# A gated linear attention and feed-forward kernel: all attention products in one block of 64x64 quarters of the array

## The chip, the cores and the metric

The kernel runs on one core of a Trainium2 chip. Its engines are called as in the profile: PE (TensorE, matmuls; PEld is its weight load), DVE (VectorE), ACT (ScalarE), POOL (GpSimd) and SP (SyncE, which here only issues transfers). The metric is the device time of one execution in microseconds, as a median over runs.

## What is computed

```python
# attention: 4 batches, 8 heads, 768 steps, head dimension 48
for t in range(S):
    state = alpha[:, :, t, :, None] * state + einsum('bhd,bhe->bhde', k[:, :, t], v[:, :, t])
    y[:, :, t] = einsum('bhd,bhde->bhe', q[:, :, t], state)
x = y.transpose(0, 2, 1, 3).reshape(3072, 384)
# feed-forward: d_model 384, d_ff 1024
out = ((x @ w1) * (x @ w2)) @ w3 @ w_out
```

The attention is a recurrence with a decay per step and dimension. The weights come as 64-bit floats and are turned into fp32 on the chip.

## The kernel before, in words

The sequence is cut into chunks of 128 steps: 6 per batch (NCH), 24 in all (N). One loop, `for n in range(N + 1)`, runs over them; its iteration n does the scores of chunk n and the output of chunk n-1, and prepares chunks n+1 to n+4. Between the attention steps it converts weights (`convert`) and, from n = 7 on, computes tiles of the first two feed-forward products (`run`, line 515, here called gate work): 3 half-tiles an iteration or fewer, and none at n = 9, 13, 17 and 21, by the table `pieces`. After the loop the feed-forward is finished: remaining gates, `w3 @ w_out` folded into one matrix, and the last product. The matmuls of line 515 make up most of the kernel.

For one chunk:
- `logs` and `decays`: logarithms of alpha (ACT), their running sums by a matmul (lines 340, 343, 346), exponentials e (ACT, 349 and 350).
- `decayed` (line 359, DVE): k and q times e, into qk. Lines 381 and 383 transpose qk on PE and copy it from PSUM to qkT (ACT). There the even head of a pair lies on partitions 0 to 47, the odd one on 64 to 111: the head's parity i sets its half of the partitions, and so its half of PE's rows. j numbers the four pairs.
- scores k times q, masked so that a query meets only keys up to its own step: up to n = 7 by full 128x128 products (line 454) and two DVE masks (457); from n = 8 (TURNED) on by quarters of the array (line 430): the block of early keys against all 128 queries and the block of late keys against the 64 late queries. An odd head's blocks lie turned by a half, and four DVE operations mask them (line 440).
- the output, in two PSUM tiles y[i]: the state of earlier chunks times q (line 474), and scores times v. The values are in the early chunks one product per head over all 128 keys (line 485). From n = 8 on the first half of the queries is done between the next chunk's scores (`attend_low`, line 419) and the second half after the transposes (line 482). A copy of the odd heads' v with its halves exchanged (vt, line 167, POOL) serves that.
- ACT copies y to x (line 489), and SP stores it to DRAM (xd) with two transfers per chunk; later x is gathered from there for the feed-forward (line 501).
- `outer` (line 393) makes the chunk's own k times v, and `advance` (lines 410 to 412, POOL) decays the state every second chunk.

All PSUM tiles come from one pool of eight banks; a bank is taken again when its readers are done. Each engine works through its instructions in order. The order written in the loop is kept on PE; the framework places the instructions of the other engines, and `issue_after` holds some back. SP issues nearly all loads in order; POOL issues the v loads of chunks 3 to 7 and the small transfers for the decay.

Of the kernel before, what the change touches and what calls it, by code (L numbers as in the profile page):

```python
# [10 lines left out]
FP32 = mybir.dt.float32  # L11
FP32R = mybir.dt.float32r
I32 = mybir.dt.int32
# [3 lines left out]
ALU = mybir.AluOpType  # L17
# [31 lines left out]
def kernel(  # L49
# [24 lines left out]
    G = 3  # L74
# [3 lines left out]
    AHEAD = 3  # L78
    LATE = 10
    PAIRED = 8  # L80
    TURNED = 8
    assert D <= DP and DM % C == 0 and DF % CW == 0 and S % C == 0 and N % G == 0
    assert DM <= 512 and TG <= 512

    def pool(name, bufs, stack=ctx, **kw):
        return stack.enter_context(tc.tile_pool(name=name, bufs=bufs, **kw))
# [34 lines left out]
    xd = [dram.tile([DM, TG], FP32, name=f"xd{g}") for g in range(NG)]  # L121
# [5 lines left out]
    vts = [p1.tile([C, NP, DP], FP32, name=f"vt{i}") for i in range(2)]  # L127
# [28 lines left out]
    def load_v(n):  # L156
        if n < N:
            st["v", n] = vs[n % len(vs)]
            (nc.gpsimd if 2 < n < 8 else nc.sync).dma_start(out=st["v", n][:, :, 0:D], in_=rows(v, n))

    def turned(n):
        return TURNED <= n < N

    def turn_v(n):
        if turned(n):
            for half in range(2):
                nc.gpsimd.tensor_copy(out=vts[n % 2][ds(DP * half, DP), :, 0:D],
                                      in_=st["v", n][ds(DP * (1 - half), DP), 1::2, 0:D])

    spare = tr[0].tile([C, 3 * KM * TG], FP32R, tag="x3", name="x3")[:].bitcast(FP32)  # L170
    sums2 = spare[:, 0:4 * C].rearrange("p (e s t) -> p e s t", e=2, s=2)
# [13 lines left out]

    w12 = [p.tile([C, 3, 2, KM, CW], FP32R, name=f"w12{i}") for i, p in enumerate((w12ap, const))]

    made = work.tile([C, 2, NP, C], FP32, tag="ms", name="ms")
    utri, after = made[:, 0, 0, :], made[:, 0, 1, :]

    sums = p1.tile([C, 2, C], FP32R, name="sums")
    signs = p1.tile([C, 2, C], FP32R, name="signs")
    keep = p1.tile([C, C], I32, name="keep")
    keep_turned = p1.tile([C, 2, DP], I32, name="keep_turned")
    qks = [p1.tile([C, 2, H, DP], FP32, name=f"qk{i}") for i in range(3)]
    Ts = [p1.tile([C, NP, DP], FP32, name=f"T{i}") for i in range(2)]
    decs = [p1.tile([C, 3, NP], FP32, name=f"dec{i}") for i in range(2)]
# [5 lines left out]
    nc.gpsimd.tensor_copy(out=sums[:, 1], in_=utri)  # L203
    nc.vector.memset(rebias, -(1023.0 - 127.0) * 2.0 ** 23)

    nc.vector.tensor_scalar_mul(keep, utri, -1.0)
    keep_bc = keep[:, None, :].to_broadcast([C, NP, C])
    for half in range(2):
        nc.gpsimd.tensor_copy(out=keep_turned[ds(DP * half, DP), 1 - half], in_=keep[ds(DP * half, DP), ds(DP * half, DP)])
    nc.gpsimd.memset(keep_turned[DP:, 1], -1)  # L210
    for x in qks:
        nc.vector.memset(x[:, :, :, D:], 0.0)
    make_identity(nc, ident)
# [55 lines left out]
    weights, begun, thirds, done = deque(), deque(), deque(), []  # L269
# [29 lines left out]
    later = deque()  # L299
# [112 lines left out]
        mark["pool"] = nc.gpsimd.tensor_tensor(Ts[0][:, :, 0:D], st.pop(("T", n - 1)),  # L412
                                               dec[:, :, None].to_broadcast([C, NP, D]), op=ALU.mult).ins

    def attend_low(n, jj, i, half):

        s, w = ds(DP * i, DP), (vts[n % 2] if i else st["v", n])
        h = half * NP // 2 + jj
        nc.tensor.matmul(st["y", n][0][i][ds(DP * half, DP), jj, 0:DP], w[s, h if i else 2 * h, :],  # L419
                         st["ms", n][s, i, h, 0:DP], start=(n % NCH == 0 and jj == 0), stop=True, skip_group_check=True)  # L420

    def turned_scores(n):

        qkT = st["qkT", n]
        sc = [bank().rearrange("p (j c) -> p j c", j=NP) for _ in range(2)]
        for j in range(NP):
            for part in range(2):
                for i in range(2):
                    r, t = ds(DP * i, D), slice(DP * part, C)
                    nc.tensor.matmul(sc[i][ds(DP * (part ^ i), DP), j, t], qkT[r, 0, j, ds(DP * part, DP)],  # L430
                                     qkT[r, 1, j, t], start=True, stop=True)
            if turned(n - 1):
                for i in range(2):
                    attend_low(n - 1, j % 2, i, i ^ (j < 2))
        ms = work.tile([C, 2, NP, C], FP32, tag="ms", name="ms")
        for i in range(2):
            r = ds(DP * i, DP)
            low, high = (keep_turned[r, 0], keep_turned[:, 1]) if i else (keep[r, 0:DP], keep[:, DP:])
            for x, mask, t in ((slice(DP * i, DP * (i + 1)), low, slice(0, DP)), (slice(0, C), high, slice(DP, C))):
                masked = nc.vector.tensor_tensor(ms[x, i, :, t].bitcast(I32), sc[i][x, :, t].bitcast(I32),  # L440
                                                 mask[:, None, :].to_broadcast([x.stop - x.start, NP, DP]),
                                                 op=ALU.bitwise_and)
        ends_of_part1[0] = mark["ms", n] = masked.ins
        st["ms", n] = ms

    def scores(n):
        if turned(n):
            return turned_scores(n)
        qkT = st["qkT", n]
        sc = [bank().rearrange("p (j c) -> p j c", j=NP) for _ in range(2)]  # L450
        for j in range(NP):
            for i in range(2):
                r = ds(DP * i, D)
                nc.tensor.matmul(sc[i][:, j, :], qkT[r, 0, j, :], qkT[r, 1, j, :], start=True, stop=True)  # L454
        ms = work.tile([C, 2, NP, C], FP32, tag="ms", name="ms")
        for i in range(2):
            masked = nc.vector.tensor_tensor(ms[:, i].bitcast(I32), sc[i].bitcast(I32), keep_bc, op=ALU.bitwise_and)  # L457
        ends_of_part1[0] = mark["ms", n] = masked.ins
        st["ms", n] = ms

    HP = NP // 2

    def attend_state(n):
        qkT = st.pop(("qkT", n))

        y = [bank()[:, 0:HP * C].rearrange("p (j c) -> p j c", c=C) for _ in range(2)]
        st["y", n] = y, [(half * HP + j, i, y[i][ds(DP * half, DP), j, :])
                         for j in range(HP) for i in range(2) for half in range(2)]  # L470
        if n % NCH:
            for j, i, to in st["y", n][1]:
                r = ds(DP * i, D)
                nc.tensor.matmul(to, Ts[n % 2][r, j, :], qkT[r, 1, j, :],  # L474
                                 start=(j % HP == 0), stop=False, skip_group_check=True)

    def attend(n):
        (y, heads), ms, vc = st.pop(("y", n)), st.pop(("ms", n)), st.pop(("v", n))
        for j, i, to in heads:
            if turned(n):  # L480
                w = vts[n % 2][:, j, :] if i else vc[:, 2 * j, :]
                nc.tensor.matmul(to[:, DP:], w, ms[:, i, j, DP:], start=False,  # L482
                                 stop=(j % HP == HP - 1), skip_group_check=True)
            else:
                nc.tensor.matmul(to, vc[:, 2 * j + i, :], ms[:, i, j, :], start=(n % NCH == 0 and j % HP == 0),  # L485
                                 stop=(j % HP == HP - 1), skip_group_check=True)
        x = work.tile([C, HP, 2, C], FP32, tag="x", name="x", bufs=4)
        for i in range(2):
            copied = nc.scalar.copy(x[:, :, i], y[i])
        ends_of_part1[1] = copied.ins  # L490
        x = x.rearrange("p j i t -> p (j i) t")

        g, c = divmod(n, G)
        to = xd[g].rearrange("(b h d) t -> b d h t", b=2, d=D)
        for half in range(2):
            later.append((to[half, :, :, ds(c * C, C)], x[ds(DP * half, D)]))


    def load_x(g, queue=nc.sync):
        st["xT", g] = xp.tile([C, KM, TG], FP32, tag="xT", name="xT")  # L500
# [27 lines left out]
    ends_of_part1 = [None, None]  # L528
    pending, late = deque(), False
# [159 lines left out]
    for n in range(N + 1):  # L689
# [14 lines left out]
                fetch(raws)  # L704
        if n >= FIRST:
            load_v(n + 2)
        if n:
            attend_state(n - 1)
        if n < N:
            scores(n)  # L710
        else:
            for j in range(NP):
                for i in range(2):
                    attend_low(n - 1, j % 2, i, i ^ (j < 2))
        transposed(n + 1)
        if n == 1:
            decays(3)
# [8 lines left out]
        if n - 2 in begin and n > FIRST:  # L726
            g, tiles = begin[n - 2]
# [16 lines left out]
        if n < N - 2 and n != FIRST:  # L744
            with after_marks(*marks):
                convert(2 if early else 1, raws)
        advance(n)
        turn_v(n)
        if n:
            attend(n - 1)  # L750
        outer(n)
        if n > FIRST:
            third(ready)
# [35 lines left out]
    late = True  # L789
# [12 lines left out]
    low, high = range(FH), range(FH, KF)  # L802
# [74 lines left out]
```

## Time and profile before

| what | us |
|---|---|
| median of 3 runs | 465.93 |
| lowest and highest | 465.54, 466.16 |
| the profiled execution | 464.49 |
| its span in the profile | 462.8 |
| masks of early chunks, DVE L457, 16 operations | 10.3 |
| masks of later chunks, DVE L440, 64 operations | 26.6 |
| vt copies, POOL L167, 32 operations | 17.8 |
| x copies, ACT L489, 48 operations | 15.7 |
| matmuls of line 515 on PE, all shapes | 346.3 |

A line of the profile's groups gives the source line, the engine, the operation, the tiles written and read, shapes and count, then busy time, mean ns of one, and the idle time just before them with what ended it. The chain of waits follows the work that ended last from its end to its start; a piece of it has a start, a length and a line. An fp32 matmul shows as two passes, so eight matmuls are x16. A timeline lists instructions by engine with start and length; lengths of neighbours overlap, since a matmul's or copy's time counts until its last write.

### The profile page before, as it was taken

What the parts mean: (1) busy time and instruction counts of PE and PEld (TensorE: products, weight loads), DVE (VectorE), ACT (ScalarE), POOL (GpSimd) and SP (SyncE); (2) the same over time, 40 slices, a digit from 0 to 9 for tenths busy, and PEclk for the clock granted to TensorE, in tenths of its full rate; (3) what the DMA queues carried; (4) which work ended last, traced back from release to release, by engine and by line L of the source; (5) the groups of instructions that cost most, each with busy time, mean ns of one, the idle gap of its engine ahead of it and who ended that gap; (6) DMA issues with size and microseconds to landing.
All of it is one profiled execution on the core that took longest, in us unless ns stands there. A gap on an engine that the chain in (4) does not pass through costs nothing.

```text
span 462.8 us, 11150 instructions
## 1 busy us (share of the span) xinstructions
PE 446.9 (97%) x4296; PEld 423.2 (91%) x4296; DVE 371.7 (80%) x610; ACT 276.4 (60%) x544; POOL 95.1 (21%) x186
## 2 busy tenths in 40 slices
PE   4998999999999999999999999999999999999996
PEld 2675699898999989999999999999999999999996
DVE  2779997999979988999998999997542967776671
ACT  4685975767658563988875676764545443333430
POOL 6234232325414430121221201212010000000000
PEclk9999999999999999999999999999999999999999
DMA  9999999999999974466856446412115875665511
GB/s 173 254 208 228 261 224 192 248 209 219 184 227 193 234 165 138 130 224 212 235 178 196 146 128 177 149 52 86 51 48 153 243 210 180 186 178 159 166 51 52
DMA packets 148869, 80.37 MB, mean 174 GB/s; under 512 B 97392, under 2 KB 138608, under 8 KB 148816
## 3 DMA queue, kind: packets, MB, share of 16 engines
q1 hardware_dynamic: 143040, 64.44, 57.3%
q0 software_dynamic: 5776, 15.22, 11.0%
q8 instruction: 34, 0.56, 0.5%
q14 instruction: 19, 0.16, 0.1%
HBM read 57.58 MB, written 22.06 MB: 172 GB/s over the span
## 4 chain that ended last, share of the span: by engine, by line
PE 88%; DVE 4%; DMA 4%; ACT 2%; issue 1%; SPq 0%; DVEq 0%; ACTq 0%
PE bank L515 72%; DMA kq<-in_q_dram 3%; PE bank L381 3%; PE bank L430 3%; PE bank L482 2%; PE bank L474 2%; PE bank L340 1%; PE bank L393 1%; PE bank L346 1%; PE bank L454 1%; PE bank L343 1%; PE bank L419 1%; DVE qk L359 1%; DVE ms L457 1%; PE bank L485 1%
## 5 line engine op out<-in xcount | busy, mean ns | idle before, releaser
L515 PE MATMUL bank<-x,w 128*128 128x384 f32 x1152 | 210.2, 337 | 1.7 <-ACT qkT L383 1.1
L515 PEld LDWEIGHTS bank<-x,w 128*128 128x128 f32 x1152 | 200.2, 188 | 4.1 <-ACT qkT L383 1.4
L515 PE MATMUL bank<-w3o,ab 128*128 128x384 f32 x576 | 100.2, 336 | 0.0
L515 PEld LDWEIGHTS bank<-w3o,ab 128*128 128x128 f32 x576 | 99.9, 188 | 0.0
L540 ACT ACTIVATE bank<-bank 128x384 f32<-128x384 f32 x96 | 45.6, 476 | 43.4 <-PE bank L515 43.1
L524 ACT ACTIVATE t<-bank 128x384 f32<-128x384 f32 x64 | 31.9, 499 | 54.9 <-PE bank L515 54.9
L590 POOL DMA_DIRECT2D abd<-ab x45 | 25.8, 573 | 137.9 <-DVE ab L576 121.3
L383 ACT COPY qkT<-bank 128x512 f32<-128x512 f32 x48 | 26.2, 596 | 24.8 <-PE bank L381 24.8
L641 DVE TENSOR_TENSOR ab<-abl,ab 128x1024 fp32r<-128x1024 f32 x24 | 29.3, 1223 | 12.3 <-ACT ab L640 12.3
L640 ACT ACTIVATE ab<-abl 128x1024 fp32r<-128x1024 f32 x24 | 25.5, 1061 | 20.2 <-PE bank L515 18.4
L515 PE MATMUL bank<-wo,w3T 128*128 128x384 f32 x192 | 35.9, 334 | 0.0
L576 DVE TENSOR_TENSOR ab<-bank,r 128x384 f32<-128x384 f32 x44 | 24.1, 548 | 12.5 <-PE bank L515 6.3
L515 PEld LDWEIGHTS bank<-wo,w3T 128*128 128x128 f32 x192 | 33.5, 188 | 0.0
L249 ACT ACTIVATE power<-power,rebias 128x512 uint32<-128x512 uint32 (+1 forms) x36 | 25.3, 701 | 12.6 <-DVE power L248 12.4
L359 DVE TENSOR_TENSOR qk<-kq,e 128x768 f32<-128x768 f32 x24 | 23.1, 964 | 11.3 <-ACT e L350 7.9
L526 DVE SCALAR_TENSOR_TENSOR o<-bank,t 128x384 f32<-128x384 f32 x24 | 13.4, 557 | 23.0 <-issue 13.7
L642 DVE SCALAR_TENSOR_TENSOR ab<-ab,abl 128x1024 fp32r<-128x1024 f32 x24 | 29.2, 1217 | 0.0
L526 DVE SCALAR_TENSOR_TENSOR r<-bank,t 128x384 f32<-128x384 f32 x40 | 22.0, 550 | 6.8 <-PE bank L515 3.4
L251 DVE SCALAR_TENSOR_TENSOR mant<-mant,rest 128x512 f32<-128x512 uint32 (+1 forms) x36 | 23.4, 649 | 3.7 <-ACT rest L244 3.7
L252 DVE SCALAR_TENSOR_TENSOR power<-raw,power 128x512 uint32<-128x512 uint32 (+1 forms) x36 | 23.5, 653 | 2.4 <-ACT power L249 2.4
L253 DVE TENSOR_TENSOR mant<-mant,power 128x512 f32<-128x512 f32 (+1 forms) x36 | 23.6, 655 | 0.5
L244 ACT ACTIVATE rest<-raw 128x512 f32<-128x512 uint32 (+1 forms) x36 | 23.3, 649 | 0.0
(102 smaller groups left out, 675.2 us busy)
## 6 DMA issues: line engine op xcount, KB each, us to landing
abl<-abd SPq DMA_DIRECT2D x24, 512.0 KB, 4.7
abd<-ab POOLq DMA_DIRECT2D x45, 192.0 KB, 3.2
raw<-in_moe_w_dram SPq DMA_DIRECT2D x64, 128.0 KB, 3.4
raw<-in_moe_w_dram SPq DMA_DIRECT2D x12, 512.0 KB, 5.8
xT<-xd POOLq DMA_DIRECT2D x9, 576.0 KB, 4.7
kq<-in_k_dram SPq DMA_DIRECT2D x24, 192.0 KB, 5.2
kq<-in_q_dram SPq DMA_DIRECT2D x24, 192.0 KB, 5.4
xd<-x SPq DMA_DIRECT2D x48, 96.0 KB, 3.9
```

The lines of the kernel that those rows point to most:

```text
L249: nc.scalar.activation(power, power, AF.Relu, scale=2.0 ** 23, bias=rebias)
L359: mark["qk", n] = nc.vector.tensor_mul(qks[n % 3][:, :, :, 0:D], st.pop(("kq", n)), st.pop(("e", n)).rearrange("p i (h d) -> p i h d", h=H ...
L383: mark["qkT", n] = nc.scalar.copy(qkT[:, :, :, ds(DP * half, DP)], tp[half]).ins
L515: nc.tensor.matmul(p, w[part][i], x[part][i], start=start and part == parts[0] and i == 0, stop=stop and part == parts[-1] and i == n - 1, ...
L524: nc.scalar.activation(t, p1, AF.Copy, scale=(1.0 + 1.0 / P) * scale)
L526: nc.vector.scalar_tensor_tensor(to, p2, scale, t, op0=ALU.mult, op1=ALU.add)
L540: nc.scalar.activation(p, p, AF.Copy, scale=1.0 + 1.0 / P)
L576: nc.vector.tensor_mul(ab, p, r[0])
L590: (nc.gpsimd if late else nc.sync).dma_start(out=abd[g][:, f, :], in_=ab)
L640: nc.scalar.activation(t[:, 0], ab, AF.Copy, scale=1.0 - 2.0 ** -13)
L641: nc.vector.tensor_sub(t[:, 1], ab, t[:, 0].bitcast(FP32))
L642: nc.vector.scalar_tensor_tensor(t[:, 2], t[:, 0].bitcast(FP32), -1.0 - 1.0 / P, ab, op0=ALU.mult, op1=ALU.add)
```

## The change

TURNED falls away; all chunks use quarters of 64x64. LQ = 3 is new. For each head pair j and parity i:
- Scores go to the quarter (i, i): rows of the parity, outputs on the parity's partitions. Early keys against all queries go to one bank (two halves e = 0 and 1 of the queries side by side), late keys against late queries to another.
- The masked scores ms have the form [128, 3, 4 pairs, 64]: first-half queries (DVE mask), second-half queries for early keys (no mask needed, an ACT copy), second-half queries for late keys (DVE mask). Both halves of the keys lie on the partitions of the head's parity.
- State and values of pairs j = 0 to 2 go to the quarters (i, 1-i) and into one PSUM tile of three pairs; those of pair 3 go to (i, i), like the scores, and into another. The values of all queries are done here, so lines 419, 482 and 485 become one place.
- `attention(n)` interleaves the two lists, state and values of pairs 0 to 2 on one side, scores of n and then state and values of pair 3 on the other, by costs 2 and 1 for 128 and 64 columns.
- vt now serves both parities: both its halves hold the other half of v, and it is made for every chunk.
- The copy to x and its store stay where the values stood in the loop. A chunk is stored with four transfers (three pairs or one pair, for each half) instead of two.

```diff
-    TURNED = 8
+    LQ = 3
     def turn_v(n):
-        if turned(n):
-            for half in range(2):
-                nc.gpsimd.tensor_copy(out=vts[n % 2][ds(DP * half, DP), :, 0:D],
-                                      in_=st["v", n][ds(DP * (1 - half), DP), 1::2, 0:D])
+        if n < N:
+            for i in range(2):
+                nc.gpsimd.tensor_copy(out=vts[n % 2][ds(DP * i, DP), :, 0:D],
+                                      in_=st["v", n][ds(DP * (1 - i), DP), i::2, 0:D])
...
+    keep = p1.tile([C, DP], I32, name="keep")
+    keep_bc = keep[:, None, :].to_broadcast([C, NP, DP])
...
+    def attend(n):
+        ms, vc, vt, qkT = st.pop(("ms", n)), st.pop(("v", n)), vts[n % 2], st.pop(("qkT", n))
+        y = [bank()[:, 0:x * C].rearrange("p (j c) -> p j c", c=C) for x in (LQ, NP - LQ)]
+        first, state = set(), n % NCH > 0
+        def add(j, i, w, x, t):
+            at = j >= LQ
+            to = y[at][ds(DP * (i if at else 1 - i), DP), j - LQ * at, t]
+            nc.tensor.matmul(to, w, x, start=(at, i) not in first, stop=True, skip_group_check=True)
+            first.add((at, i))
+        def steps(heads):
+            for j in heads * state:
+                yield 2, [(j, i, Ts[n % 2][ds(DP * i, D), j, :], qkT[ds(DP * i, D), 1, j, :], slice(0, C)) for i in range(2)]
+            for j in heads:
+                yield 2, [(j, i, vt[DP:, j, :] if i else vc[0:DP, 2 * j, :], ms[ds(DP * i, DP), 0:2, j, :], slice(0, C))
+                          for i in range(2)]
+            for j in heads:
+                yield 1, [(j, i, vc[DP:, 2 * j + 1, :] if i else vt[0:DP, j, :], ms[ds(DP * i, DP), 2, j, :], slice(DP, C))
+                          for i in range(2)]
...
+        def copied():
+            x = work.tile([C, NP, C], FP32, tag="x", name="x", bufs=4)
+            for a, b in zip(y, (x[:, 0:LQ], x[:, LQ:])):
+                ends_of_part1[1] = nc.scalar.copy(b, a).ins
+            g, c = divmod(n, G)
+            to = xd[g].rearrange("(j i d) t -> i d j t", i=2, d=D)[:, :, :, ds(c * C, C)]
+            for half in range(2):
+                s = ds(DP * half, D)
+                later.append((to[1 - half, :, 0:LQ], x[s, 0:LQ]))
+                later.append((to[half, :, LQ:], x[s, LQ:]))
...
+    def scores(n):
+        qkT = st["qkT", n]
+        sc = [bank().rearrange("p (e j c) -> p e j c", e=2, j=NP), bank()[:, 0:NP * DP].rearrange("p (j c) -> p j c", j=NP)]
+        def score(x):
+            j, late = x
+            for i in range(2):
+                r, to = ds(DP * i, D), ds(DP * i, DP)
+                q = qkT[r, 1, j, ds(DP * late, DP)] if late else qkT[r, 1, j, :].rearrange("p (e c) -> p e c", e=2)
+                nc.tensor.matmul(sc[1][to, j, :] if late else sc[0][to, :, j, :], qkT[r, 0, j, ds(DP * late, DP)], q,
+                                 start=True, stop=True)
+        def masked():
+            ms = st["ms", n] = work.tile([C, 3, NP, DP], FP32, tag="ms", name="ms")
+            for e, x in ((0, sc[0][:, 0]), (2, sc[1])):
+                last = nc.vector.tensor_tensor(ms[:, e].bitcast(I32), x.bitcast(I32), keep_bc, op=ALU.bitwise_and)
+            mark["ms", n] = ends_of_part1[0] = last.ins
+            nc.scalar.copy(ms[:, 1], sc[0][:, 1])
+        return [(2 - late, score, (j, late)) for j in range(NP) for late in range(2)], masked
+    def attention(n):
+        low, high = attend(n - 1) if n else ([], [])
+        done = None
+        if n < N:
+            own, done = scores(n)
+            high = own + high
+        low, high, at = deque(low), deque(high), [0, 0]
+        while low or high:
+            k = 0 if not high or low and at[0] <= at[1] else 1
+            cost, f, x = (low, high)[k].popleft()
+            at[k] += cost
+            f(x)
+        if done:
+            done()
...
-        if n:
-            attend_state(n - 1)
-        if n < N:
-            scores(n)
...
+        attention(n)
         transposed(n + 1)
...
         advance(n)
         turn_v(n)
         if n:
-            attend(n - 1)
+            st.pop(("x", n - 1))()
         outer(n)
```

More of the change, by code (lines that the diff above doesn't have):

```diff
@@ L159, in load_v @@
             (nc.gpsimd if 2 < n < 8 else nc.sync).dma_start(out=st["v", n][:, :, 0:D], in_=rows(v, n))
-    def turned(n):
-        return TURNED <= n < N
     def turn_v(n):
-        if turned(n):
-            for half in range(2):
-                nc.gpsimd.tensor_copy(out=vts[n % 2][ds(DP * half, DP), :, 0:D],
-                                      in_=st["v", n][ds(DP * (1 - half), DP), 1::2, 0:D])
+        if n < N:
+            for i in range(2):
+                nc.gpsimd.tensor_copy(out=vts[n % 2][ds(DP * i, DP), :, 0:D],
+                                      in_=st["v", n][ds(DP * (1 - i), DP), i::2, 0:D])
     spare = tr[0].tile([C, 3 * KM * TG], FP32R, tag="x3", name="x3")[:].bitcast(FP32)
@@ L186 @@
     w12 = [p.tile([C, 3, 2, KM, CW], FP32R, name=f"w12{i}") for i, p in enumerate((w12ap, const))]
-    made = work.tile([C, 2, NP, C], FP32, tag="ms", name="ms")
-    utri, after = made[:, 0, 0, :], made[:, 0, 1, :]
+    made = work.tile([C, 3, NP, DP], FP32, tag="ms", name="ms").rearrange("p a j c -> p (a j c)")
+    utri, after = made[:, 0:C], made[:, C:2 * C]
     sums = p1.tile([C, 2, C], FP32R, name="sums")
     signs = p1.tile([C, 2, C], FP32R, name="signs")
-    keep = p1.tile([C, C], I32, name="keep")
-    keep_turned = p1.tile([C, 2, DP], I32, name="keep_turned")
+    keep = p1.tile([C, DP], I32, name="keep")
     qks = [p1.tile([C, 2, H, DP], FP32, name=f"qk{i}") for i in range(3)]
@@ L204 @@
     nc.vector.memset(rebias, -(1023.0 - 127.0) * 2.0 ** 23)
[L206 to L210, printed above, removed]
+    for i in range(2):
+        nc.vector.tensor_scalar_mul(keep[ds(DP * i, DP)], utri[ds(DP * i, DP), ds(DP * i, DP)], -1.0)
+    keep_bc = keep[:, None, :].to_broadcast([C, NP, DP])
     for x in qks:
@@ L413, in advance @@
                                                dec[:, :, None].to_broadcast([C, NP, D]), op=ALU.mult).ins
[L415 to L422, printed above, removed]
-        qkT = st["qkT", n]
[L425 to L451, printed above, removed]
-            for i in range(2):
[L453 to L496, printed above, removed]
+    def attend(n):
[16 more added lines that the diff above has]
+                          for i in range(2)]
+        def act(x):
+            for y in x:
+                add(*y)
+        def copied():
[8 more added lines that the diff above has]
+                later.append((to[half, :, LQ:], x[s, LQ:]))
+        st["x", n] = copied
+        return *([(k, act, x) for k, x in steps(list(h))] for h in (range(LQ), range(LQ, NP))),
@@ L706 @@
             load_v(n + 2)
-        if n:
-            attend_state(n - 1)
-        if n < N:
-            scores(n)
[L711 to L714, printed above, removed]
+        attention(n)
         transposed(n + 1)
```

## Prediction

> **What bounds the kernel.** I read the page's busy times first, then its forty slices, then the chain that ended last.
>
> ```profile
> PE 446.9 (97%) x4296; PEld 423.2 (91%) x4296; DVE 371.7 (80%) x610; ACT 276.4 (60%) x544; POOL 95.1 (21%) x186
> ...
> PE   4998999999999999999999999999999999999996
> ...
> DVE  2779997999979988999998999997542967776671
> ...
> PE 88%; DVE 4%; DMA 4%; ACT 2%; issue 1%; SPq 0%; DVEq 0%; ACTq 0%
> ```
>
> PE is busy 446.9 of 462.8 us and holds 88% of the chain; its granted clock is 1.0 in every slice. From 184 us on, PE runs the feed-forward without a gap (30.0 of 30.0 us in each stretch up to 430), and the change doesn't touch that. So the question is how much earlier the last attention (n = 24, at 183 us) is done. A table of busy time by stretch gives PE's idle time before: 9.7 us in 0:50, 0.3 in 50:70, 1.1 in 70:90, 0.6 in 90:130, none in 130:170, 0.5 in 170:190. After 50 us, PE work removed is time won, unless a new wait eats it. Before 50 us something else decides:
>
> ```profile
> 39.74 7.11 DMA kq<-in_q_dram
> 46.97 0.96 DVE qk L359
> 47.93 1.20 DVE ms L457 x2
> ```
>
> In this stage the chain runs from a load of k and q over VectorE's work (the masks included) to the next load; PE is not in it.
>
> **PE's work per chunk.** The chain of one full iteration (n = 15), with start, length and what ran:
>
> ```profile
> 119.48 0.60 PE bank L474 x16
> ...
> 121.19 0.64 PE bank L381 x16
> 121.83 0.61 PE bank L482 x16
> 122.45 0.45 PE bank L393 x16
> 122.90 0.71 PE bank L515 x3
> ```
>
> Each fp32 matmul counts as two passes. L474 (state: N=128, four passes on each of four quarters) takes 0.60; L485 (values of early chunks: N=128, eight passes on each column half) takes 1.02 in the chain. So four passes of 128 cost 0.42, one 0.105, and the start-up is 0.18. L482 (N=64, eight passes per half) takes 0.61: a pass of 64 costs (0.61-0.18)/8 = 0.054. Test: scores and first-half values (120.08 to 121.19, 1.11 us) put 8 passes of 128 and 4 of 64 on the quarters (i,i): 0.84+0.22 = 1.06, so I add 0.05 to a block.
>
> Before, a full iteration costs 0.60+1.11+0.61 = 2.32 us; 0.15 of L482's 0.61 is start-up after the transposes that L393 will pay in its place, so 2.17. After: the apart heads (LQ = 3) hold (3+3) matmuls of 128 and 3 of 64 on (i,1-i): 12x0.105+6x0.054 = 1.58; the quarters (i,i) hold four scores, one state, one value of 128 and 4+1 of 64: 12x0.105+10x0.054 = 1.80, plus 0.18+0.05 = 2.03 us. Won: 0.14. The sum over iterations:
> - full ones (n = 9 to 12, 14 to 18, 20 to 23): 13x0.14 = 1.8 won.
> - n = 13 and 19 (first chunk of a batch, no state): before 1.25 (147.64 to 148.89) +0.46; after 10x0.105+10x0.054+0.23 = 1.82. Lost 0.1 each.
> - n = 24 (no scores to fill the other quarters): before 0.60+0.29+0.62 = 1.51, after 1.58+0.18 = 1.76. Lost 0.25.
> - n = 6, 7, 8, whose values are the 1.02 form (scores before: L454, 1.09 in the chain, or 0.87 at n = 8): 0.60+1.09+1.02-0.15 = 2.56 against 2.03, 1.09+1.02-0.15 = 1.96 against 1.82, 0.60+0.87+1.02-0.15 = 2.34 against 2.03. Rounded down 0.45, 0.15 and 0.3 won.
>
> Together 2.25 us off PE.
>
> **Stalls that go.** PE's longest idle after 50 us:
>
> ```profile
> 83.97 1.32 PE L515 MATMUL bank<-x,w 128*128 128x384 f32 x6
> 86.39 1.84 PE L515 MATMUL bank<-x,w 128*128 128x384 f32 x9 [1.10 <-ACT qkT L383]
> ```
>
> It waits for a PSUM bank that the qkT copy frees; that copy stood behind a power step (L249), which waited for VectorE. In the built order of the changed kernel the bank needed there is freed by the x copy, which stands ahead of that step: I take the 1.1 as gone. VectorE gets shorter too: the masks of a chunk go from four operations (L440: 408+406+428+425 ns) to two of 128x256 (about 406 each), 0.85 us less. I take as gone also the 0.5 at 109.8 and 110.8 and the 0.55 at 171.9 (which waited for a mask). Sum 2.1.
>
> **Waits that come.** The third quarter of the scores needs no mask and is copied by ScalarE (128x256 from PSUM like L489, 384 ns alone, about 0.3 in a row). It lies in the bank of the first mask, and in the built order the copy waits for that mask. Mostly ScalarE's queue then holds: this copy, two x copies (0.65 together), two qkT copies (1.0). Before, the x copies stood after qkT, because the values came later. So qkT, which the next scores need, stands behind VectorE's mask. It hurts where no gate work lies between two attentions (pieces 0: n = 9, 13, 17, 21). VectorE, then ScalarE, around n = 17:
>
> ```profile
> 136.69 0.96 DVE L359 TENSOR_TENSOR qk<-kq,e 128x768 f32<-128x768 f32 x1
> 137.56 0.74 DVE L440 TENSOR_TENSOR ms<-bank,keep 64x256 int32<-64x256 int32 x2
> ```
>
> ```profile
> 137.66 1.08 ACT L383 COPY qkT<-bank 128x512 f32<-128x512 f32 x2 [1.01 <-PE bank L381]
> 138.62 1.18 ACT L507 ACTIVATE x<-xT 128x1152 fp32r<-128x1152 f32 x1
> 139.69 0.65 ACT L489 COPY x<-bank 128x256 f32<-128x256 f32 x2
> ```
>
> The mask comes after qk, as it still does: first mask done 137.93, copy 138.2, x 138.9, qkT 139.9. PE starts this attention at 135.2, ends it at 137.25, transposes until 137.95 and is at the next scores, after L346, at 138.4: it waits 1.5 us. In the same way n = 21 (first mask 165.1 to 165.5, qkT 167.4, PE there at 166.6): 0.85; n = 9 (mask 78.5 to 78.9): 0.4; n = 13, where the x copies stand first: 0.4. Sum 3.1. At n = 6 the mask is late (54.11): scores(7) gain nothing, 0.4 of the 2.25 is lost.
>
> The Trainium skill speaks against this placing: "PSUM — Partial Sum Buffer", section "PSUM bank collisions raise a hardware error", says that the scheduler orders any two instructions of different engines on the same bank and partition quadrant, even two reads. No row of before shows a bank read by both engines. By the rule n = 17 costs the 1.5 above; were the copy free of it, qkT would be done near 139.2 and cost 0.8.
>
> **Costed at nothing, with their cover.** Two POOL copies (L167, 557 ns each) are added in each of n = 0 to 7, and the state product of n = 4 (43.3 us) moves about 1 us back; VectorE's mask at 47.85 waits for the k and q load (landed 46.85), which covers it; uncovered it is 1 us, once. SP issues four xd stores per chunk instead of two, the same bytes; SP's k, q and v loads behind them lie two or more chunks ahead, and the gather of x reads a group whose last store is two iterations old. If a load came late behind two more issues, one iteration would lose a part of the 3.9 us to landing. The early masks shrink from 1.20 to about 0.75 in the loop shown; two loops would give 0.9, and as ScalarE's longer queue takes part of it I count 0.5.
>
> **Sum.** -2.25 -2.1 +3.1 +0.4 -0.5 = -1.35 us. The profiled execution took 464.49 (span 462.8), so 463.1; it lies 1.4 below the median 465.93 of the runs, on which the same step gives 464.6.
>
> **Rivals.**
> - The new waits are hidden (masks come earlier, since VectorE loses 0.85 us a chunk in stretches where it is 97% busy, such as 90:130): 3.1 and 0.4 fall away, 461.1. For: that share. Against: the mask at n = 17 waits on qk, which follows PE's own pace.
> - Gain and waits cancel within 0.9 us: 465.9.
> - Slower, by ScalarE's queue in the gate iterations as well (n = 11, 12, 14, 15, 16, 19, 20, 23). After an attention PE has transposes (0.74), L393 (0.45) and nine gate matmuls (1.64) before it needs a bank from this queue, 2.8 us; the copy is done 0.7 after the mask starts. It decides from a mask 2.1 us late. Before, masks start 2.3 us late at n = 11 (92.26 to 94.55), 1.5 at 12, 2.1 at 14, 2.2 at 19. If relief doesn't come and ScalarE's lateness feeds back into VectorE, some 0.6 us in each of eight: +4.8-1.35, 469.4. Against: the same 0.85 us.
> - Both row halves of the array now write one bank (different partitions), which no row of before shows; L474 kept each row half to its bank. If they took turns, a block of 2.03 would be about 3.8: 18 iterations x 1.8, 498 us. The skill's page "TensorEngine Tiling (Array Packing)", "Gotcha 1: PSUM Pressure", says that different row tiles cannot access one bank at once; by that the sum would be this 498. Bounds of the unknown: 0 and +32 us; I take 0, since the two column halves of L482 already share a bank at full pace.
>
> **Chances.** Forecast (463.3 to 465.0) 0.33; waits hidden 0.20; cancelled 0.18; ScalarE's queue 0.26; taking turns 0.03. Faster by over 0.2% (0.93 us, about what a measurement of this kernel can tell from no change) 0.53, within 0.18, slower 0.29. The range takes half of the hidden case and most of the queue case: 461.8 to 468.6.
>
> **What would show it.** The attention block between two gate groups, at 2.0 us against 1.71+0.46 (2.6 would mean poor packing); no group like L482 after the transposes; VectorE's masks near 20 us in all instead of 37; the 1.1 us before the gate matmuls near 86 us gone; PE waiting for qkT at the scores of n = 18 and 22 by about 1.5 and 0.9. Wrong if those waits are absent, if banks from ScalarE's copies hold L515 in gate iterations, or if the passes of (0,0) and (1,1) no longer overlap.

## The result, and the profile after

The changed kernel took 473.88 us (median of six runs, 471.62 to 475.36), the one before 466.05 in the same count of runs: a ratio of 1.0163, 95% interval 1.0132 to 1.0195, or 7.6 us lost where 1.35 were forecast as won. The profiled execution took 471.62 (span 469.4). Its page, busy times, two of the forty-slice rows and the chain:

```profile
PE 447.8 (95%) x4552; PEld 424.6 (90%) x4552; DVE 357.2 (76%) x579; ACT 281.9 (60%) x568; POOL 104.2 (22%) x199
...
PE   4988899998998999999999999999999999999996
...
PEclk9989999999999999999999999999999999999999
...
PE 67%; DMA 10%; DVE 6%; ACT 5%; issue 3%; SPq 2%; POOL 1%; ACTq 0%; POOLq 0%; DVEq 0%
```

VectorE did get lighter (372 to 357 us), yet PE holds 67% of the chain instead of 88%; transfers have 10% and SP's queue, which had none, 2%. From the last attention on nothing changed: after it PE needs 274.46 us in both kernels, and 274.46 or 274.50 in all kernels below but one (b_four_vfirst, 275.44). So all of the loss lies before it. The last attention ended at 184.64 us before and at 191.27 after.

PE's waits of the changed kernel (line waited at, what ended the wait, us in all, times, longest; waits of 4.6 us at L337 and 2.0 at L375 stand in this view too, and the kernel before has them as 5.0 and 2.3):

```profile
PE bank L458 <- ACT qkT L377: 3.5, 3, 1.3
PE bank L334 <- ACT x L310: 2.4, 1, 2.4
...
PE bank L418 <- POOL T L406: 1.7, 1, 1.7
PE bank L502 <- ACT ms L466: 1.5, 2, 1.0
PE bank L387 <- DMA v<-in_v_dram: 1.0, 2, 0.7
```

And the waits of the other engines:

```profile
ACT ms L466 <- DVE ms L464: 36.9, 20, 3.6
POOL vt L164 <- DMA v<-in_v_dram: 32.2, 10, 6.6
```

The first of these two is the queue the prediction priced: ScalarE's new copy (L466) waits for VectorE's mask. The second, 13.1 us in 6 before, belongs to the vt copies, which it priced at nothing. The 2.4 us at L334 lie near 24 us, and something follows them that no slice of before shows. Stretches of 1 us (busy time of PE and of the other engines, then PE's granted clock, DMA share, GB/s):

```profile
24.00:25.00 1.00, 0.00 (x0) 0.00 (x0) 1.00 (x3) 1.00 (x3) 0.69 (x2) 1.00 0.81 158
25.00:26.00 1.00, 0.52 (x1) 0.50 (x2) 0.79 (x1) 1.00 (x2) 0.00 (x0) 0.54 0.94 167
26.00:27.00 1.00, 1.00 (x3) 0.41 (x2) 0.90 (x2) 0.04 (x1) 0.00 (x0) 0.50 0.98 197
...
28.00:29.00 1.00, 1.00 (x25) 0.66 (x28) 0.00 (x0) 0.51 (x2) 0.00 (x0) 0.76 1.03 329
29.00:30.00 1.00, 1.00 (x56) 1.00 (x52) 0.11 (x1) 0.88 (x2) 0.88 (x3) 1.00 1.29 243
```

PE stood still from 23.04 to 25.48, and from 25.1 on its granted clock is 0.5 for 3.4 us.

### The profile page after: what moved, and what is told of

It is laid out like the page before. It is cut to its first block, busy times and chain, and to the rows that moved or that the text cites. A ratio compares the mean times of both kernels' runs of the same rounds, so it can differ in the third digit from the quotient of the medians.

```text
span 469.4 us, 11758 instructions
## 1 busy us (share of the span) xinstructions
PE 447.8 (95%) x4552; PEld 424.6 (90%) x4552; DVE 357.2 (76%) x579; ACT 281.9 (60%) x568; POOL 104.2 (22%) x199
## 4 chain that ended last, share of the span: by engine, by line
PE 67%; DMA 10%; DVE 6%; ACT 5%; issue 3%; SPq 2%; POOL 1%; ACTq 0%; POOLq 0%; DVEq 0%
PE bank L502 64%; DMA ac<-in_alpha_dram 3%; DMA v<-in_v_dram 2%; DMA xd<-x 2%; DVE qk L353 2%; ACT qkT L377 1%; DMA dec<-ends 1%; PE bank L418 1%; SPq L299 1%; DMA abd<-ab 1%; ACT x L438 1%; DMA ends<-e 1%; DVE ms L464 1%; SPq L154 1%; DVE r L513 1%
## 5 line engine op out<-in xcount | busy, mean ns | idle before, releaser
L502 PE MATMUL bank<-x,w 128*128 128x384 f32 x1152 | 209.6, 337 | 1.5 <-ACT ms L466 1.5
L502 PEld LDWEIGHTS bank<-x,w 128*128 128x128 f32 x1152 | 200.1, 188 | 3.6 <-ACT ms L466 2.4
L502 PE MATMUL bank<-w3o,ab 128*128 128x384 f32 x576 | 100.2, 336 | 0.0
L502 PEld LDWEIGHTS bank<-w3o,ab 128*128 128x128 f32 x576 | 99.9, 188 | 0.0
L527 ACT ACTIVATE bank<-bank 128x384 f32<-128x384 f32 x96 | 45.8, 477 | 39.4 <-PE bank L502 39.3
L511 ACT ACTIVATE t<-bank 128x384 f32<-128x384 f32 x64 | 31.4, 503 | 47.4 <-PE bank L502 45.3
L458 PE MATMUL bank<-qkT 48*64 48x128 f32 (+1 forms) x768 | 38.9, 252 | 3.7 <-ACT qkT L377 3.5
L458 PEld LDWEIGHTS bank<-qkT 48*64 48x64 f32 x768 | 35.3, 137 | 6.0 <-ACT qkT L377 5.9
L418 PE MATMUL bank<-ms,v 64*64 64x64 f32 (+1 forms) x384 | 37.1, 245 | 0.4 <-ACT ms L466 0.4
L418 PE MATMUL bank<-ms,vt 64*64 64x64 f32 (+1 forms) x384 | 36.6, 245 | 0.0
L502 PE MATMUL bank<-wo,w3T 128*128 128x384 f32 x192 | 35.8, 334 | 0.0
L418 PEld LDWEIGHTS bank<-ms,v 64*64 64x64 f32 x384 | 34.2, 133 | 1.5 <-ACT ms L466 0.6
L164 POOL COPY vt<-v 64x192 f32<-64x192 f32 x48 | 26.6, 554 | 37.6 <-DMA v<-in_v_dram 32.2
L418 PEld LDWEIGHTS bank<-ms,vt 64*64 64x64 f32 x384 | 33.8, 133 | 0.0
L502 PEld LDWEIGHTS bank<-wo,w3T 128*128 128x128 f32 x192 | 33.5, 188 | 0.0
L466 ACT COPY ms<-bank 128x256 f32<-128x256 f32 x24 | 8.9, 371 | 36.9 <-DVE ms L464 36.9
## 6 DMA issues: line engine op xcount, KB each, us to landing
raw<-in_moe_w_dram SPq DMA_DIRECT2D x64, 128.0 KB, 3.4
```

Of the source, the lines that this page charges most:

```text
L164: nc.gpsimd.tensor_copy(out=vts[n % 2][ds(DP * i, DP), :, 0:D], in_=st["v", n][ds(DP * (1 - i), DP), i::2, 0:D])
L418: nc.tensor.matmul(to, w, x, start=(at, i) not in first, stop=True, skip_group_check=True)
L458: nc.tensor.matmul(sc[1][to, j, :] if late else sc[0][to, :, j, :], qkT[r, 0, j, ds(DP * late, DP)], q, start=True, stop=True)
L502: nc.tensor.matmul(p, w[part][i], x[part][i], start=start and part == parts[0] and i == 0, stop=stop and part == parts[-1] and i == n - 1, ...
L511: nc.scalar.activation(t, p1, AF.Copy, scale=(1.0 + 1.0 / P) * scale)
L527: nc.scalar.activation(p, p, AF.Copy, scale=1.0 + 1.0 / P)
```

## The experiments

Four theories were held: **queue** (ScalarE's copy behind the mask holds x and qkT back), **stores** (SP's 48 more issues), **POOL** (vt copies in chunks 0 to 7) and, from the first results on, **clock** (a PE gap halves the clock). The table gives each ratio against the kernel before, and two readings of the one profiled execution: when the transposes of chunk 8 end (the early part), and the time from there to the end of the last attention (the late part) less what the lowered clock took there, worked out as the sum of 1 minus the granted clock over stretches of 1 us.

| kernel | ratio (95% interval) | early | of it clock | late, clock taken off |
|---|---|---|---|---|
| before | | 57.75 | 0 | 126.9 |
| changed | 1.0163 (1.0132 to 1.0195) | 60.84 | 1.7 | 130.4 |
| b_four | 1.0120 (1.0084 to 1.0157) | 59.27 | 0 | 130.1 |
| b_vt | 1.0092 (1.0058 to 1.0126) | 62.05 | 3.4 | 126.1 |
| a_two | 1.0213 (1.0174 to 1.0252) | 63.76 | 5.1 | 129.6 |
| a_dve | 1.0177 (1.0137 to 1.0216) | 58.71 | 0 | 130.5 |
| h_late | 1.0107 (1.0064 to 1.0150) | 58.54 | 0 | 128.9 |
| h_early | 1.0117 (1.0091 to 1.0142) | 63.21 | 3.4 | 126.7 |
| a_swap | 1.0083 (1.0048 to 1.0118) | 64.05 | 0 | 126.2 |
| h_late2 | 1.0021 (1.0005 to 1.0036) | 58.98 | 3.4 | 128.0 |
| a_queue | 1.0219 (1.0192 to 1.0247) | 64.67 | 1.7 | 129.1 |
| a_swap_queue | 1.0163 (1.0133 to 1.0193) | 60.09 | 0 | 127.6 |
| h_early_queue | 1.0112 (1.0085 to 1.0139) | 61.63 | 1.7 | 127.3 |
| late_queue | 1.0031 (1.0011 to 1.0051) | 57.01 | 0 | 128.8 |
| a_novt | 1.0140 (1.0080 to 1.0200) | 61.36 | 5.1 | 127.9 |
| a_swap_novt | 1.0035 (1.0001 to 1.0069) | 59.86 | 1.7 | 126.6 |
| a_swap_vtdve | 1.0173 (1.0119 to 1.0227) | 66.36 | 3.4 | 126.4 |
| a_fix | 1.0173 (1.0122 to 1.0224) | 67.32 | 3.4 | 126.2 |
| h_late_vfirst | 1.0039 (1.0020 to 1.0058) | 57.77 | 0 | 127.5 |
| b_four_vfirst | 1.0093 (1.0063 to 1.0123) | 59.64 | 0 | 127.3 |

One profile is one execution; the early column above all differs between executions of one kernel, so the ratios decide and the columns say where to look.

**One suspect at a time.** b_four and b_vt put one part of the change into the kernel before:

```diff
 b_four
-            later.append((to[half, :, :, ds(c * C, C)], x[ds(DP * half, D)]))
+            for h in (slice(0, 3), slice(3, None)):
+                later.append((to[half, :, h, ds(c * C, C)], x[ds(DP * half, D), h]))
 b_vt, in turn_v
-        if turned(n):
+        if n < N:
```

> The kernel before with its two xd stores per chunk issued as four (heads of one half split three and one, the same bytes). STORES theory (SP's 48 more issues of about 0.4 us, in order, delay the loads and gate stores behind them, and this carries most of the loss): 1.010 to 1.016 of before, with PE's new idle time late in part 1. QUEUE theory (ScalarE's copy behind VectorE's mask holds x, x, qkT, qkT back): 0.999 to 1.003.

> The kernel before with POOL's two vt copies issued in chunks 0 to 7 as well (nothing reads them there). POOL theory (these copies, which wait for the v loads, delay POOL's decay work in the first 60 us): 1.003 to 1.006, lost before 60 us. STORES and QUEUE theories: 0.999 to 1.002.

Both suspects cost time alone and in the old kernel: b_four 1.012, as its theory said, and b_vt 1.009, more than the 1.003 to 1.006 of its theory. SP's queue in the kernel before, and in b_four (start, length of the issue):

```profile
103.72 0.91 SPq L305 DMA_DIRECT2D xd<-x  x2
...
107.34 0.64 SPq L159 DMA_DIRECT2D v<-in_v_dram  x1
...
110.27 0.95 SPq L305 DMA_DIRECT2D xd<-x  x2
```

```profile
107.24 1.91 SPq L305 DMA_DIRECT2D xd<-x  x4
...
111.94 0.83 SPq L159 DMA_DIRECT2D v<-in_v_dram  x1
...
114.03 2.65 SPq L305 DMA_DIRECT2D xd<-x  x4
```

The same v load leaves at 107.34 before and at 111.94 in b_four, though the attention of chunk 13 is only 1.3 us later there (107.49 against 106.20). SP has next to no slack at this place: an issue starts as the last one ends. PE's timeline of b_four shows who pays:

```profile
117.14 0.67 PE L393 MATMUL bank<-v,qk 128*64 128x48 f32 x16 [2.56 <-DMA v<-in_v_dram]
```

In the changed kernel this load leaves at 113.00, and its chain runs through it:

```profile
113.00 4.37 DMA v<-in_v_dram
...
117.42 0.67 PE bank L387 x16
```

b_vt pays early. PE's longest waits of b_vt; before, the second was 0.8 in one:

```profile
PE bank L343 <- ACT la L324: 4.5, 1, 4.5
PE bank L474 <- POOL T L412: 4.5, 2, 3.8
```

The 3.8 us ended at 33.66, and the clock then fell to 0.5 for 6.8 us. The ten runs of b_vt go with their mean clock: 464.77 us at 1.0 (the time of before), 471.53 at 0.989, 471.66 and 471.66 at 0.985. 1.5% of 470 us are 7.0; the difference is 6.9. Not every kernel goes so: h_late2's four runs at 1.0 took 465.44 to 466.69 us, its two at 0.991 466.84 and 467.07; and of the 82 runs of the kernel before on record the 53 at 0.999 or more have a median of 464.5, the eight at 0.993 or less one of 465.8. A lowered clock can thus cost much less than its share.

a_two saves the two stores with one more copy on ScalarE per chunk; a_dve moves the new copy from ScalarE to VectorE:

```diff
 a_two
-            for a, b in zip(y, (x[:, 0:LQ], x[:, LQ:])):
-                ends_of_part1[1] = nc.scalar.copy(b, a).ins
+            nc.scalar.copy(x[:, 0:LQ], y[0])
+            for i in range(2):
+                ends_of_part1[1] = nc.scalar.copy(x[ds(DP * i, DP), LQ:], y[1][ds(DP * (1 - i), DP)]).ins
...
-                later.append((to[1 - half, :, 0:LQ], x[s, 0:LQ]))
-                later.append((to[half, :, LQ:], x[s, LQ:]))
+                later.append((to[1 - half], x[s]))
 a_dve
-            nc.scalar.copy(ms[:, 1], sc[0][:, 1])
+            nc.vector.tensor_copy(out=ms[:, 1], in_=sc[0][:, 1])
```

> The changed kernel with the copy of the fourth head pair turned (two 64-partition copies, each to the other half), so that x holds the heads of a parity on one half and two xd stores per chunk are enough; ScalarE has one more small copy per chunk. STORES theory: 1.002 to 1.007 of before (most of the 7.6 us comes back). QUEUE theory: 1.014 to 1.020, since the queue behind the mask is the same and one copy longer.

> The changed kernel with the copy of the unmasked quarter of the scores on VectorE behind its two masks (plus 0.4 us of VectorE per chunk), so that ScalarE's x and qkT copies no longer stand behind a mask. QUEUE theory: the long attention blocks after a chunk without gate work (2.5 to 4.9 us against 2.1 in the profile of the changed kernel, 8 us in sum) go back to about 2.1: 0.998 to 1.005 of before. STORES theory: 1.012 to 1.018.

Neither helps. a_two lost 8.5 us of its profile to the clock (after gaps of 3.0, 1.8 and 2.4 us) and PE's waits for qkT rose from 3.5 to 5.8 us with the third copy on ScalarE, so it can't judge the stores. a_dve shortens the long attention blocks in part (chunk 18: 2.79 us against 4.87), but PE waits 3.2 us for the v load near 120 us, and as long at L502 for ScalarE (L511) from 89.8: other waits took the place of these.

**Early half, late half.** h_late has the old form in chunks 0 to 7 and the new one from 8 on; h_early the reverse; h_late2 and a_swap have two stores per chunk, with the rows of the last two heads left exchanged:

```diff
+    def new(n):
+        return n >= 8        # h_late, h_late2; h_early: n < 8
...
 a_swap, h_late2
-                later.append((to[1 - half, :, 0:LQ], x[s, 0:LQ]))
-                later.append((to[half, :, LQ:], x[s, LQ:]))
+                later.append((to[1 - half], x[s]))
```

> Chunks 0 to 7 in the form of before, chunks 8 to 23 in the changed form (four xd stores for each of these). EARLY CLOCK theory (the changed form makes PE idle 2.4 to 3.0 us near 23 us, and after such a gap the granted clock is 0.5 for 3.4 or 6.8 us; this, with what follows early, is half of the loss): the mean clock is back at 0.998 to 1.0 and the time 1.003 to 1.009 of before. If the loss is late work alone (the queue behind the mask, the stores): 1.012 to 1.017.

> Chunks 0 to 7 in the changed form, chunks 8 to 23 in the form of before (two stores each). EARLY CLOCK theory: 1.005 to 1.011 of before, mean clock 0.985 to 0.996, a PE gap of over 2 us near 23 us followed by a clock of 0.5. If the loss is late work alone: 1.000 to 1.003.

> The changed kernel with two xd stores per chunk instead of four, and nothing else moved: the rows of the last two heads land exchanged in xd, so the output is that of a layer with these two heads' rows exchanged. STORES theory: SP's v loads come 1.0 to 1.3 us earlier per chunk, the v wait of 0.7 us near 117 us goes, the time is 1.005 to 1.010 of before. QUEUE theory: 1.013 to 1.018. If the clock decides, the time follows the mean clock (about 4.7 us for each 0.01), whatever SP does.

> Both: chunks 0 to 7 as before, chunks 8 to 23 changed with two stores each (the last two heads' rows of these chunks land exchanged in xd, so the output is that of a layer with them exchanged). If early clock and stores carry the loss: 0.994 to 1.002 of before, what is left being ScalarE's queue behind the mask. If this queue carries it: 1.006 to 1.012, with attention blocks of 2.5 to 3.5 us after chunks without gate work.

The loss has two halves, 1.0107 and 1.0117 by themselves; together that is more than the 1.0163 of the whole, so they don't simply add up. Two stores bring the late half to 1.0021 and the whole change to 1.0083; the late column of a_swap is 126.2, below before's 126.9. Most of the late half is thus the stores, though h_late2's own late column, 128.0, stays 1.1 above before's. The early half stays: h_early has PE gaps of 2.4 us at 20.3 and 39.3, each with a lowered clock behind it. The waits they belong to (line numbers differ between the kernels; L431 does the state and the values here, L347 the running sums):

```profile
PE bank L431 <- POOL vt L170: 2.8, 2, 2.4
PE bank L347 <- ACT x L323: 2.4, 1, 2.4
```

The gap at 20.3 is the wait for ScalarE (L323), which is left open below; the one at 39.3 is the wait for a vt copy. The chain of waits up to it:

```profile
13.57 4.51 DMA v<-in_v_dram
...
18.14 0.57 POOL vt L170
18.70 3.73 DMA ends<-e
...
23.06 0.72 POOL dec L374
23.78 5.51 DMA dec<-ends
...
31.92 0.53 POOL T L419
...
33.58 5.88 DMA ends<-e
```

A vt copy on POOL waits for its v load; behind it stands POOL's issue that writes the decay values (ends), then the one that reads them back (dec), then the state T, which PE's state product needs (1.5 us of waiting at 31.0); and the next vt copy stands behind the next dec issue, which waits for its ends. It is a chain of transfers of 3.7 to 5.9 us each, and a copy that waits ahead of one of its issues lengthens it.

**ScalarE's queue.** The order of before is put back: qkT first, then the new copy, then x.

```diff
-            nc.scalar.copy(ms[:, 1], sc[0][:, 1])
+            st["mc"] = lambda: nc.scalar.copy(ms[:, 1], sc[0][:, 1])
...
         transposed(n + 1)
+        if "mc" in st:
+            with after_marks(*[("qkT", n + 1)] * (n < N - 1)):
+                st.pop("mc")()
...
-            st.pop(("x", n - 1))()
+            with after_marks(*[("qkT", n + 1)] * (n < N - 1)):
+                st.pop(("x", n - 1))()
```

> The changed kernel with ScalarE's queue put in the order of before: the qkT copies first, then the copy of the unmasked quarter, then the x copies (four stores stay). QUEUE theory (qkT behind a copy that waits for VectorE's mask makes the 2.4 us PE gap near 23 us, with the clock at 0.5 behind it, and the long attention blocks at chunks 10, 14, 18, 22): 1.005 to 1.011 of before, the blocks of 2.5 to 4.9 us back at 2.1 to 2.4 but for the v waits. STORES theory alone: 1.012 to 1.019.

> The same queue order with two stores per chunk (the last two heads' rows land exchanged in xd, and the output is that of a layer with them exchanged). If stores and queue together carry the loss: 0.997 to 1.003 of before, with the mean clock at 0.997 or more. If POOL's vt copies in chunks 0 to 7 carry a part of it by the clock: 1.004 to 1.009, mean clock 0.990 to 0.995.

> Only chunks 0 to 7 in the changed form, with ScalarE's queue in the order of before and two stores per chunk (the last two heads' rows of these chunks land exchanged in xd). QUEUE theory for the early part: 0.999 to 1.004 of before, no PE gap over 2 us before 30 us. POOL theory (vt copies): 1.006 to 1.011 with a clock of 0.5 after a gap before 50 us, as in the kernel of before with these copies.

> Chunks 0 to 7 as before, chunks 8 to 23 changed with ScalarE's queue in the order of before and, from chunk 9 on, two stores per chunk; the exchanged rows of the last two heads are put right by loading x in four pieces, so the output is the reference's. QUEUE and STORES theories: the late loss is gone and PE's 0.05 us per full attention and VectorE's shorter masks are left: 0.994 to 1.000 of before. If the queue had no part in the late loss: 1.001 to 1.004, as without the new order.

The queue theory falls as the main cause. The order does what it should to the waits it names: in chunks 10, 14, 18 and 22 the attention blocks are 2.19, 2.31, 2.79 and 2.74 us long, against 2.52, 4.10, 4.87 and 3.10 (2.12 is a block without waits). That is 4.6 us less of waiting, but the late part is only 1.4 shorter with four stores and 1.4 longer with two. In a_queue's timeline the next wait is 2.34 us, at L387 from 119.28 to 121.62; the profile names the copy L466, but the v load had left only at 116.36, and POOL, which waited for it too, started in the same moment as PE:

```profile
121.64 1.35 POOL L164 COPY vt<-v 64x192 f32<-64x192 f32 x2 [4.74 <-DMA v<-in_v_dram]
```

The early part isn't mended by this order at all (a gap of 2.4 to 2.6 us between 20 and 26 us stays in all three kernels that have it; h_early_queue's 1.0112 is at the upper end of what the POOL theory gave it), and x copied later means stores issued later. a_queue and a_swap_queue lie above all their expectations. late_queue, which loads x in four pieces to put the exchanged rows right, is no better than h_late2; its 1.0031 is what was expected if the queue had no part in the late loss.

**POOL's copies out.** a_novt leaves them out in chunks 0 to 7, a_swap_novt both these and two of the stores; the other two move them to VectorE:

```diff
 a_novt, a_swap_novt
-        nc.gpsimd.memset(x[:, :, D:], 0.0)
+        nc.gpsimd.memset(x, 0.0)
...
-        if n < N:
+        if 8 <= n < N:
 a_swap_vtdve, a_fix
-                nc.gpsimd.tensor_copy(out=vts[n % 2][ds(DP * i, DP), :, 0:D],
+                (nc.vector if n < 8 else nc.gpsimd).tensor_copy(out=vts[n % 2][ds(DP * i, DP), :, 0:D],
```

> The changed kernel without POOL's vt copies in chunks 0 to 7 (these chunks read zeros in their place, so their output lacks half of the values' part); four stores stay. POOL theory for the early part (the copies wait for v loads ahead of the issues that bring the decay vector, and these cost the early 2 to 4 us and the clock at 0.5): 1.006 to 1.011 of before, the loss of the stores alone, and the transposes of chunk 8 end near 59 us instead of 60.8 to 64.7. If the early loss is ScalarE's queue or the stores: 1.014 to 1.018.

> The same with two stores per chunk (the last two heads' rows exchanged besides). If POOL's copies and SP's stores together carry the whole loss: 0.996 to 1.001 of before, and the transposes of chunk 8 end by 59 us. If something third (ScalarE's queue, the packing) has a part: 1.004 to 1.009.

> The changed kernel with two stores per chunk (the last two heads' rows exchanged in xd) and the vt copies of chunks 0 to 7 on VectorE instead of POOL. POOL theory: 0.997 to 1.004 of before (VectorE is 67% busy in 0 to 60 us, and two copies a chunk cost it some 0.5 us each chunk). If it is the wait for the v load that hurts, on whichever engine the copies stand: 1.006 to 1.012.

> The whole change with both mended: vt copies of chunks 0 to 7 on VectorE, two stores per chunk, the exchanged rows put right by loading x in four pieces (three more issues for each of the five loads that SP makes in part 1), so the output is the reference's. STORES and POOL theories: 0.997 to 1.005 of before, at most 0.003 above the same kernel with the rows left exchanged. If neither is the cause: 1.008 to 1.018.

Without copies and extra stores 1.0163 becomes 1.0035 (1.0001 to 1.0069). These intervals lie apart, so the two together carry most of the loss. How it divides between them is less sure: the interval of a_swap_novt overlaps a_swap's, and a_novt alone, 1.0140 (1.0080 to 1.0200), can't be told from the whole change. It lies at the edge of the expectation for another cause; all four of its runs have a mean clock of 0.985 (6.8 us lost in the profile). What the copies cost by themselves is shown in the old kernel alone, by b_vt.

On VectorE the copies bring the early part to 66 to 67 us. Of this 5.1 us are lost at the very start. The chain of a_swap_vtdve:

```profile
3.84 4.56 DMA v<-in_v_dram
8.42 0.07 DVE vt L164
...
9.27 0.30 POOL sums L198
9.61 1.66 PE bank L337 x2
```

VectorE's vt copy of chunk 0 waits for its v load ahead of a constant that the first matmul needs, so PE starts at 9.61 us; in a_swap it starts at 4.53. A second such wait lasts from 33.62 to 39.05, with masks and qk behind it. So a copy that waits for a load at the head of a queue hurts on VectorE too. Without the 5.1 us the early part would be 61.3, an estimate, against a_swap's 64.05; the copy of chunk 0 behind the constants wasn't tried, so whether VectorE would serve for the copies stays open. a_fix, the whole change with the output of the reference, starts as late (9.44) and gains nothing in all, though its late part is 126.2.

**Which load the stores hold back.** Both kernels move only the v load, from iteration 6 on, ahead of the stores and of the alpha, k and q loads of its iteration:

```diff
+        if n >= FIRST:
+            load_v(n + 2)
         if not 1 < n < FIRST:
             store()
...
-        if n >= FIRST:
-            load_v(n + 2)
```

> Chunks 0 to 7 as before, chunks 8 to 23 changed with four stores, and from chunk 6 on the v load issued by SP ahead of the stores and the alpha, k and q loads of its iteration instead of behind them. If the stores hurt by holding back the v load alone: 1.001 to 1.005 of before (1.011 without this order). If they hurt by SP's time and its places in flight as a whole, so that alpha, k or q is late in v's place: 1.008 to 1.013.

> The kernel before with four stores per chunk and the v load first in the same way. If the v load alone is what the stores delay: 1.002 to 1.006 of before (1.012 without this order; what is left lies before chunk 6, where the order isn't changed). If SP's time as a whole counts: 1.009 to 1.015.

1.0107 becomes 1.0039, as expected if the v load alone is held back: in the late half of the change it is the v load's place. b_four's late part falls from 130.1 to 127.3, with 126.9 before, but its ratio only to 1.0093, which was expected if SP's time as a whole counts. Its early part, where the order isn't changed, keeps its stores, its profile lost 1.0 us after the last attention, and some of its runs had a clock of 0.989; so there the v load's part rests on one profile. The kernel before with the v load first and its two stores wasn't run. No version was faster than the kernel before.

## Why the prediction was wrong, point by point

- **The step that failed** is the paragraph "Costed at nothing, with their cover", twice. It held that "SP's k, q and v loads behind them lie two or more chunks ahead", and that a late load would lose "a part of the 3.9 us to landing" in one iteration. (The 3.9 us are the store's median; the v loads that SP issues took 4.8.) Two chunks ahead in program order is nothing where SP issues without a pause: two more issues of 0.42 us (median of L299) in every chunk, with their waits, made one v load leave 3.3 us (b_four) and 3.6 us (the changed kernel) later, counted from the attention of chunk 13, and cost 3.2 us in the late part by b_four, 4.2 by a_swap. And the "Two POOL copies" with "1 us, once" cost 0.9% by themselves in b_vt. The cover named, a k and q load, doesn't reach POOL's queue: the copies wait for v at the head of it, ahead of the decay transfers, and the state product named there waited 1.7 us for T instead of 0.8.
- **Left out altogether:** what follows a gap in the clock. Gaps were priced by their length. The changed kernel's six runs have mean clocks of 0.989 to 0.996, which would be 3.4 us on average at full price; how much of it reached the time isn't known (b_vt paid the full price, h_late2 about 1 us of 4).
- **PE's work**, forecast at 2.25 us won, was right. Start and length of the first matmuls of an attention and of the first one behind its block, in a full iteration without waits, before (n = 15) and after (n = 16):

```profile
119.41 0.67 PE L474 MATMUL bank<-qkT,T 48*64 48x128 f32 x16
...
122.83 0.44 PE L515 MATMUL bank<-x,w 128*128 128x384 f32 x1
```

```profile
132.15 0.33 PE L418 MATMUL bank<-qkT,T 48*64 48x128 f32 x2
...
135.45 0.44 PE L502 MATMUL bank<-x,w 128*128 128x384 f32 x1
```

That is 3.42 us before and 3.30 after: 0.12 won, 0.14 forecast. Where L393 doesn't follow at once (n = 11, 17 and 23) it is 0.26. Chunks 13 and 19 lost 0.1 each, as forecast, the last 0.31 instead of 0.25; with 0.7 for chunks 6 to 8 the sum is 2.2 us. The 0.05 us per full attention in an expectation above compares a block's 2.12 us, from the first matmul to the end of the last, with 2.17 from a chain that counts to the next start; counted so, the block takes 2.06.
- **Waits that come**, forecast at 3.1: the blocks of chunks 10, 14, 18, 22 are 0.4, 2.0, 2.75 and 1.0 us too long, 6.1 in all, against 0.4, 0.4, 1.5 and 0.85. The mechanism was right, the place too, the size half of what came. With two stores (a_swap) these blocks are still 2.9, 5.8 (1.7 of it by the clock), 3.6 and 3.1 us long, and yet its late part is below before's: they aren't what decides. At chunk 18 the mask itself was late (VectorE's L550 ahead of it waited 0.8 us for a gate store that SP had issued at 136.6), so a part of this may be the stores again. Chunk 6 lost 1.5, not 0.4.
- **Stalls that go**: the 1.1 us at 86 went, but 1.0 at 89.8 came, at L502 behind the new copy; the one near 110 turned into the long block of chunk 14.
- **Masks**: 48 of 415 ns are 19.9 us, as forecast (20).
- **The rivals.** Slower was there at 0.29, by ScalarE's queue in gate iterations; that isn't what decided: its sign, gate work held by a bank from ScalarE's copy, came to 1.5 us in two waits (L502) instead of 4.8, and the queue's order could be changed and the loss stayed. Taking turns in a bank is refuted: it would have been 3.8 us a block, and 2.12 were measured, so the rule cited there from "TensorEngine Tiling (Array Packing)" differs from this run. The order of two engines on one bank, cited from "PSUM — Partial Sum Buffer", agrees: ScalarE's copy, which needs no mask, waited 36.9 us for VectorE's masks.
- **What stays open:** the last 0.35%. In the changed early form PE waits 2.1 to 3.0 us at L334 (behind ScalarE's L310) between 20 and 28 us, in every kernel that has this form, with or without vt copies (2.38 in a_swap_novt, with the lowered clock behind it). In the timeline ScalarE stands there before a weight conversion (L254) that waits for VectorE and precedes qkT; in the kernel before it comes after qkT. That this order is the cause was only argued; it wasn't tried.

## What to carry to other kernels

Before a step is priced at nothing on an in-order queue, look at that queue's own timeline: if one issue starts where the last one ends, the load that is next needed pays for every issue put before it, and moving that load ahead did about as much here as saving the issues (1.0039 and 1.0021, intervals that overlap). Look also at what stands behind a copy that waits for a load: here a chain of small transfers on POOL, and a constant on VectorE. And a PE gap of over 2 us can cost more than its length: two in three of them were followed here by a lowered clock, which took up to 1.7 or 3.4 us more.

## What the runs showed of the hardware

**The clock comes back in steps.** In the nineteen profiles after the one of before there are 25 stretches at a granted clock of 0.5. Nineteen are 3.41 us long and six 6.83, whatever the gap before them: 1.7 or 3.4 us of PE's work each, at most. Of 23 gaps of over 2 us, 15 were followed by one; of 49 of 1 to 2 us (without the 1.96 us that every kernel has at its start), ten. The shortest gap that was is 1.10 us (h_late, at 141.4), and 2.88 us passed without (a_swap, at 46.3). From b_vt, the end of a gap and what follows it:

```profile
32.00:33.00 1.00, 0.00 (x0) 0.00 (x0) 0.00 (x0) 0.28 (x1) 0.38 (x2) 1.00 1.20 276
33.00:34.00 1.00, 0.34 (x8) 0.34 (x12) 0.36 (x2) 1.00 (x4) 0.86 (x3) 0.73 1.05 238
34.00:35.00 1.00, 1.00 (x18) 0.67 (x12) 1.00 (x2) 0.80 (x2) 0.94 (x3) 0.50 0.94 273
...
40.00:41.00 1.00, 1.00 (x10) 0.71 (x8) 0.57 (x2) 0.60 (x2) 0.90 (x4) 0.85 1.05 321
41.00:42.00 1.00, 1.00 (x5) 0.57 (x3) 0.99 (x2) 0.04 (x1) 0.66 (x1) 1.00 1.36 224
```

The Trainium skill, "TensorE: Matmul & The Clock Gate", section "What's actually happening", has a window of 3413 ns that runs freely and decides on half or full clock; the lengths agree with it. Its rule that the clock falls after an idle window of about 3.4 us doesn't: here gaps a third as long came before such a stretch at times, and the mean clocks of one kernel's runs differ (b_vt, 0.985 to 1.0).
